# Gated FFT filter and state-space mixer on one core: first token results in freed rows of x, decay tables emitted earlier, a doubled recurrence PSUM, a narrower table and an earlier diagonal

## The chip, the cores and the metric

The kernel runs on one core of a Trainium2 chip. The metric is the device time in microseconds (us) of one execution, lower is better. A profiled execution also has a span, from the first to the last recorded instruction, which is about 1.8 us shorter than its device time.

## The reference, cut to what matters

```python
# x: [1, 2048, 1024] bfloat16
g = sigmoid((x * gate_w).sum(-1, keepdims=True))
a = irfft2(rfft2(x) * (w_r + 1j * w_i))             # A: filter over tokens and features
# B: state-space recurrence over the 2048 tokens, 1024 complex states
Bu = x @ B_bar.T
h[t] = Lam_bar * h[t - 1] + Bu[t]
b = 2.0 * (h @ Cmat.T).real + x * Dskip
return g * a + (1 - g) * b
```

## The kernel before

TensorE, VectorE and ScalarE run in an order fixed by the program text (`manual_schedule` names these three engines). The SyncE queue is not among them: it issues its transfers one after another in an order that the build chose. In the kernel before, the store of A1(9) is written two steps ahead of the first transpose of C, and the trace shows it issued behind all sixteen. The parts that matter:

- *Front, 16 steps.* Step j transforms group j of x (its 128 rows 16p + j) along the features (`fd`, PSUM `ps_fd`), ScalarE copies it out (`X1`), a first token stage follows (`s1`, PSUM `ps_s`), and its result `A1` is stored to DRAM for the next stage.
- *Recurrence, 16 units.* Each unit is two half units of 32 matmuls (PSUM `psu`), each copied to SBUF by ScalarE; then VectorE rotates, scans and rotates back.
- *Bcol*, a small table that VectorE makes and that TensorE's product `zps` reads, after the front.
- *Early output tiles* `ps_y`, which start with a product with the diagonal table `dgD`.

```python
CT = [ctp.tile([P, 8, D], BF16, name=f"CT{ri}") for ri in range(2)]
xn = [CT[i // 4][:, 2 * (i % 4):2 * (i % 4) + 2, :] for i in range(8)]   # x lies here first, C^T later
psA = ...tile_pool(name="psA", bufs=2, space=PSUM)     # ps_fd, ps_s and others
psF = ...tile_pool(name="psF", bufs=1, space=PSUM)     # psu of the first units
psX = ...tile_pool(name="psX", bufs=2, space=PSUM)     # turns of x
# [cut]
def s1(j):
    X1 = X1s.pop(j)
    psa = psA.tile([P, 2, K], FP32, name="ps_s1", tag="ps")
    for r in range(2):
        for g in range(2):
            half = slice(64 * g, 64 * (g + 1))
            nc.tensor.matmul(psa[:, g, :], lhsT=T2_sb[half, j, r, :], rhs=X1[half, r, :], ...)
    A1 = A1_4[:, j % 4]                                # four buffers, used in turn
    (nc.vector.tensor_copy if j < 8 else nc.scalar.copy)(out=A1, in_=psa)
    nc.sync.dma_start(out=t1_w[j], in_=A1)             # its place in the SyncE queue is chosen by the build
    if j % 4 == 0 and j:
        keep_A1(j - 4)                                 # column 0 of four results
# [cut] the loop over the front
    if j >= 8:
        halves(ssm, 1)                                 # one half unit of matmuls
    if j >= 9:
        vector(4.2)                                    # some VectorE pieces of the recurrence
    if j == 11:
        xctx.close()                                   # psF and psX end
        pools["u"] = ...tile_pool(name="psU", bufs=2, space=PSUM)
# [cut] after the front
for v, n in (("w", 4), ("a", 1), ...):
    assert step() == v                                 # "a": Bcol, "z": zps
    for i in range(n):
        halves(ssm, 1)
        vector(3.0)
        if v == "w" and i == 1:
            nc.vector.tensor_mul(out=fft["dgD"], ...)
```

## Time and profile before

| | before |
|---|---|
| median of the three timed runs | 346.62 us (346.26 to 347.94) |
| profiled execution | 348.02 us, span 346.2 us, mean granted clock 0.993 |
| TensorE busy | 328.4 us, 95% of the span |
| longest TensorE gap after the start | 3.39 us, at 44.98 us |
| next | 1.94 us, for `dgD`, at 105.47 us |

The chain that ended last is TensorE in 73% of its length, so the busy shares say little more than "TensorE". The useful question is where TensorE does not work, and the view of busy time by stretches answers it. The columns are the stretch, its length, then busy time and instructions of each engine, the granted clock (TensorE's clock as a share of its full one), the DMA share (rough, it can exceed 1) and the rate in GB/s. Two stretches of the kernel before:

```profile
40.00:60.00 20.00, 15.68 (x104) 9.68 (x105) 10.05 (x22) 11.06 (x17) 1.83 (x3) 0.91 1.08 212
...
80.00:110.00 30.00, 27.96 (x228) 20.00 (x229) 29.00 (x43) 10.22 (x12) 0.00 (x0) 1.00 0.71 186
```

In the first stretch TensorE (15.68 of 20 us, at a granted clock of 0.91) and VectorE (10.05 of 20 us) both stand still for part of the time. In the second TensorE loses 2.0 us while VectorE is full.

### The profile page before, as it was taken

The numbers are of one execution on the slowest core, as the hardware profiler recorded it, in microseconds if no ns is written. First come the engines' busy times: TensorE is split into PE (matmuls) and PEld (weight loads), VectorE is DVE, ScalarE is ACT, GpSimd is POOL, SyncE is SP. The second block draws the span as 40 slices with busy tenths as digits, with TensorE's granted clock in tenths as the row PEclk, the third lists the DMA queues.
The fourth block names the chain that finished last, engine by engine and source line by source line (L and its number), as shares of the span: only waits on it lengthen the run. The fifth ranks groups of instructions, "written<-read, shape, count | busy, mean of one in ns | idle before, by whom it ended". The sixth has DMA issues, their size and how long they took to land.

```text
span 346.2 us, 6210 instructions
## 1 busy us (share of the span) xinstructions
PE 328.4 (95%) x2414; PEld 213.7 (62%) x2446; DVE 289.0 (83%) x447; ACT 169.8 (49%) x214; POOL 33.6 (10%) x64
## 2 busy tenths in 40 slices
PE   8989578999998999999999999999999999999995
PEld 4445255666865775665748475858955885665552
DVE  2659356999999998999999999999990797999951
ACT  3698558775341225566646562456631333424410
POOL 1382010230000000000000000000000002112220
PEclk9999989999999999999999999999999999999999
DMA  7999999999882123889989953967302109956695
GB/s 251 407 224 130 220 220 211 214 151 252 278 196 35 61 91 92 225 225 249 276 182 287 271 170 95 247 158 203 91 2 91 62 0 149 181 98 98 113 141 166
DMA packets 83582, 58.97 MB, mean 170 GB/s; under 512 B 54329, under 2 KB 74305, under 8 KB 83425
## 3 DMA queue, kind: packets, MB, share of 16 engines
q1 hardware_dynamic: 80304, 55.90, 65.1%
q0 software_dynamic: 3168, 2.66, 7.9%
q8 instruction: 19, 0.31, 0.4%
q14 instruction: 11, 0.08, 0.1%
q10 hardware_dynamic: 80, 0.01, 0.0%
HBM read 30.76 MB, written 17.83 MB: 140 GB/s over the span
## 4 chain that ended last, share of the span: by engine, by line
PE 73%; DVE 17%; ACT 4%; SPq 2%; issue 2%; DMA 1%; DVEq 0%; ACTq 0%
PE ps_y L567 27%; PE psu L300 23%; PE ps_h L567 4%; DVE h L275 4%; PE ps_id L598 4%; PE ps_is L481 2%; SPq L205 2%; PE ps_is L506 2%; PE ps_is L482 2%; PE ps_y L571 2%; PE ps_s L457 2%; PE ps_fd L336 2%; PE psw L668 1%; DVE h L287 1%; ACT xQ L654 1%
## 5 line engine op out<-in xcount | busy, mean ns | idle before, releaser
L300 PE MATMUL psu<-xQ,BT 128*128 128x256 bf16 x1024 | 117.5, 274 | 1.5 <-ACT h L302 1.0
L300 PEld LDWEIGHTS <-BT 128*128 128x128 bf16 x1024 | 99.5, 98 | 19.1 <-issue 4.8
L567 PE MATMUL ps_y<-CT,h 128*128 128x512 bf16 x436 | 99.5, 379 | 0.6
L567 PEld LDWEIGHTS <-h 128*128 128x128 bf16 x512 | 49.5, 98 | 55.3
L275 DVE TENSOR_TENSOR_SCAN h<-rz,h 128x1024 bf16<-128x1024 f32 x32 | 72.6, 2293 | 0.3
L302 ACT CAST h<-psu 128x1024 bf16<-128x1024 f32 x32 | 32.4, 1011 | 58.2 <-PE psu L300 58.2
L613 POOL DMA_DIRECT2D BT<-y_scratch x10 | 11.9, 1194 | 241.1 <-DVE BT L607 233.5
L585 ACT ACTIVATE ye<-ps_y,omg 128x512 f32<-128x512 f32 x20 | 12.7, 684 | 43.5 <-PE ps_y L571 28.7
L336 PE MATMUL ps_fd<-G_sb,preT 128*128 128x512 bf16 x119 | 29.3, 379 | 2.9 <-ACT X L339 2.4
L262 DVE TENSOR_TENSOR su<-h,tab 128x2048 bf16<-128x2048 bf16 x16 | 19.6, 1222 | 3.5 <-ACT h L302 2.8
L336 PEld LDWEIGHTS <-preT 128*128 128x128 bf16 x128 | 12.1, 97 | 15.9 <-issue 3.8
L459 ACT CAST X<-ps_s 128x1024 bf16<-128x1024 f32 x16 | 16.2, 1015 | 8.7 <-PE ps_s L457 8.7
L287 DVE TENSOR_TENSOR h<-h,tab 128x2048 bf16<-128x2048 bf16 x16 | 20.0, 1249 | 0.5
L263 DVE TENSOR_TENSOR h<-h,tab 128x2048 bf16<-128x2048 bf16 x16 | 19.6, 1225 | 0.8
L339 ACT CAST X<-ps_fd 128x1024 bf16<-128x1024 f32 x16 | 16.2, 1013 | 8.1 <-PE ps_fd L336 7.4
L286 DVE TENSOR_TENSOR sg<-h,tab 128x2048 bf16<-128x2048 bf16 x16 | 19.5, 1219 | 0.1
L351 DVE CAST A<-ps_s 128x1024 bf16<-128x1024 f32 x8 | 9.8, 1222 | 8.6 <-DMA turn_scratch<-A 6.8
L654 ACT COPY xQ<-pt 128x1024 bf16<-128x1024 bf16 x16 | 15.8, 1020 | 1.8 <-PE pt L653 1.7
L508 ACT CAST ZT<-ps_is 128x1024 bf16<-128x1024 f32 x16 | 15.5, 1023 | 2.2 <-PE ps_is L506 2.2
L484 ACT CAST C<-ps_is 128x1024 bf16<-128x1024 f32 x16 | 16.1, 1008 | 0.0
L598 PE MATMUL ps_id<-raw,ZT 128*128 128x256 bf16 x128 | 15.9, 273 | 0.0
L567 PE MATMUL ps_h<-CT,h 128*128 128x512 bf16 x62 | 14.4, 379 | 0.1
(184 smaller groups left out, 364.7 us busy)
## 6 DMA issues: line engine op xcount, KB each, us to landing
y_scratch<-ye SPq DMA_DIRECT2D x20, 256.0 KB, 2.8
CT<-in_A_x_dram SPq DMA_DIRECT2D x8, 512.0 KB, 6.2
turn_scratch<-A SPq DMA_DIRECT2D x16, 256.0 KB, 3.7
Bb<-turn_scratch SPq DMA_DIRECT2D x16, 256.0 KB, 3.8
turn_scratch<-C SPq DMA_DIRECT2D x16, 256.0 KB, 3.6
raw<-turn_scratch SPq DMA_DIRECT2D x16, 256.0 KB, 4.0
Wb<-in_A_w_r_dram SPq DMA_DIRECT2D x32, 127.8 KB, 4.0
Wb<-in_A_w_i_dram SPq DMA_DIRECT2D x32, 127.8 KB, 3.7
```

The lines of the kernel that those rows point to most:

```text
L262: nc.vector.tensor_mul(out=su, in0=u[:, ::-1], in1=bc(1))
L263: nc.vector.tensor_mul(out=u, in0=u, in1=bc(0))
L275: nc.vector.tensor_tensor_scan(out=seg, data0=rz[:, js].rearrange("p j t -> p (j t)"), data1=seg, initial=0.0, op0=ALU.mult, op1=ALU.add)
L286: nc.vector.tensor_mul(out=sg, in0=u[:, ::-1], in1=bc(3))
L287: nc.vector.tensor_mul(out=u, in0=u, in1=bc(2))
L300: nc.tensor.matmul(psu[:, j, :], lhsT=BT[4 * q + j][:, ri, d8, :], rhs=x_t[:, d8, :, :, 8 * c:8 * (c + 1)], start=(d8 == 0), stop=(d8 == 7))
L302: nc.scalar.copy(out=u[:, ri].rearrange("p b (q j) -> p b q j", j=32), in_=psu.rearrange("p b (j q) -> p b q j", j=32))
L336: nc.tensor.matmul(ps[:, cls, :], lhsT=preTs[j][:, 4 * cls + d4, :], rhs=G_sb[:, cls, d4, :], start=(d4 == 0), stop=(d4 == 3))
L339: nc.scalar.copy(out=X1.rearrange("p r (i c) -> p r i c", c=2), in_=ps.rearrange("p c (r i) -> p r i c", r=2))
L567: nc.tensor.matmul(psy, lhsT=hs[c, jb // 4][:, ri, jb % 4, P * tq:P * (tq + 1)], rhs=CT[ri][:, jb, 512 * dh:512 * (dh + 1)], start=(i == 0 ...
L598: nc.tensor.matmul(pse[:, slot, :], lhsT=ZT_t[:, i, tb, :], rhs=fft["Gi"][:, i, :], start=(kb == 0), stop=(kb == 1))
L654: nc.scalar.copy(out=xQ[:, :, j, :].rearrange("p d (g q) -> p d g q", g=2), in_=pt.rearrange("p d (q g) -> p d g q", g=2))
```

## The change

The intent: let no store hold up the front, load less, and take two smaller waits away. Five edits:

1. Results of steps 0 to 7 go into rows of x that have been turned already (`CT[0]`), so that no result has to wait for an older one's store.
2. The decay tables `rz` are emitted on GpSimd right after their input.
3. The recurrence gets two PSUM buffers at step 7, before its first unit, instead of step 11; the gate's sums move to another pool for that.
4. The table T2 has 192 columns instead of 256 for each step, as one of its four blocks of 64 columns stood there twice.
5. The diagonal table `dgD` is made earlier on VectorE.

```diff
-        T2=b16(np.stack([np.concatenate([Tc, -Ts], axis=2), np.concatenate([Ts, Tc], axis=2)], axis=2)),
+        T2=b16(np.concatenate([Ts, Tc, -Ts], axis=2)),
 [cut: the rz copies move from the table builder to just after r_sb]
-                    nc.tensor.matmul(psa[:, g, :], lhsT=T2_sb[half, j, r, :], rhs=X1[half, r, :],
+                    nc.tensor.matmul(psa[:, g, :], lhsT=T2_sb[half, j, 64 - 64 * r:192 - 64 * r], rhs=X1[half, r, :],
-            A1 = A1_4[:, j % 4]
+            A1 = CT[0][:, j, :].rearrange("p (g k) -> p g k", g=2) if j < 8 else A1_4[:, j % 4]
-            if j % 4 == 0 and j:
+            if j in (8, 12):
                 keep_A1(j - 4)
         def keep_A1(j):
+            if j < 8:
+                nc.vector.tensor_copy(out=Acol[:, :, 0:8].rearrange("p g j -> p j g"), in_=CT[0][:, :, 0:D:K])
+                return
-        zps = psX.tile([P, K], FP32, name="zps_g", tag="pt")
+        zps = psA.tile([P, K], FP32, name="zps_g", tag="ps")
-        if j == 11:
+        if j == 7:
             xctx.close()
+            if v == "w" and i == 0:
+                nc.vector.tensor_mul(out=fft["dgD"], ...)
             halves(ssm, 1)
             vector(3.0)
-            if v == "w" and i == 1:
-                nc.vector.tensor_mul(out=fft["dgD"], ...)
```

More of the change, by code (lines that the diff above doesn't have):

```diff
@@ L191 @@
     raw = t3p.tile([P, 6 * D], BF16, name="raw")
-    fft["T2"] = raw[:, 0:4 * D].rearrange("p (j t m) -> p j t m", t=2, m=P)
+    fft["T2"] = raw[:, 0:3 * D].rearrange("p (j m) -> p j m", m=192)
     def load_x(i):
@@ L213, in make_tab @@
             nc.vector.tensor_scalar_mul(out=ang[:, j], in0=tau_f, scalar1=thp[:, 2 * jp + j:2 * jp + j + 1])
-            jb = 2 * jp + j
-            nc.gpsimd.tensor_copy(out=rz[:, jb, :], in_=r_sb[:, jb:jb + 1].to_broadcast([P, TC]))
-            nc.gpsimd.memset(rz[:, jb, 0:1], 0.0)
         sn_f = tmp.tile(sh, FP32, name="sn_f")
@@ L804 @@
     nc.scalar.activation(out=r_sb, in_=are, func=ACT.Exp)
+    for jb in range(8):
+        nc.gpsimd.tensor_copy(out=rz[:, jb, :], in_=r_sb[:, jb:jb + 1].to_broadcast([P, TC]))
+        nc.gpsimd.memset(rz[:, jb, 0:1], 0.0)
     tau_f = tmp.tile([P, TC], FP32, name="tau_f")
@@ L877 @@
         for i in range(n):
+            if v == "w" and i == 0:
+                nc.vector.tensor_mul(out=fft["dgD"], in0=ident.unsqueeze(1).to_broadcast([P, 8, P]),
+                                     in1=vecT[:, 3].unsqueeze(2).to_broadcast([P, 8, P]))
             if v == "w" and i == 3:
@@ L881 @@
             vector(3.0)
-            if v == "w" and i == 1:
-                nc.vector.tensor_mul(out=fft["dgD"], in0=ident.unsqueeze(1).to_broadcast([P, 8, P]),
-                                     in1=vecT[:, 3].unsqueeze(2).to_broadcast([P, 8, P]))
     for g in range(16):
```

## The prediction

> **What bounds the kernel now.** I read the page first (busy shares, the 40 slices, the chain that ended last), then the TensorE timeline with its gaps, then VectorE, ScalarE and the SyncE queue in the same windows. From the page, busy time and the engine shares of the chain:
>
> ```profile
> PE 328.4 (95%) x2414; PEld 213.7 (62%) x2446; DVE 289.0 (83%) x447; ACT 169.8 (49%) x214; POOL 33.6 (10%) x64
> ...
> PE 73%; DVE 17%; ACT 4%; SPq 2%; issue 2%; DMA 1%; DVEq 0%; ACTq 0%
> ```
>
> TensorE does work in 328.4 of 346.2 us, so all its gaps together are 17.8 us. In time order the chain is TensorE alone from 105.5 us to the end (in all that time the only listed waits are 0.53 and 0.23 us), and a mixture of VectorE, ScalarE and a DMA between 12 and 105 us. So what counts is by how much TensorE is shifted to the left by the time it reaches 105 us, and whether it keeps that afterwards. TensorE between 37 and 57 us (start, duration, operation, in brackets the idle before it and what ended it):
>
> ```profile
> 37.65 0.61 PE L348 MATMUL ps_s<-X,raw 64*128 64x512 bf16 x4
> 39.71 1.89 PE L336 MATMUL ps_fd<-G_sb,preT 128*128 128x512 bf16 x8 [1.45 <-ACT X L339]
> 44.98 1.04 PE L348 MATMUL ps_s<-X,raw 64*128 64x512 bf16 x4 [3.39 <-DVE A L351]
> 45.95 4.64 PE L300 MATMUL psu<-xQ,BT 128*128 128x256 bf16 x32
> 50.43 1.89 PE L336 MATMUL ps_fd<-G_sb,preT 128*128 128x512 bf16 x7
> 52.25 0.60 PE L348 MATMUL ps_s<-X,raw 64*128 64x512 bf16 x4
> 53.58 3.65 PE L300 MATMUL psu<-xQ,BT 128*128 128x256 bf16 x32 [0.73 <-ACT h L302]
> ```
>
> The largest gap of the kernel, 3.39 us, waits for VectorE to empty the other PSUM buffer. The VectorE and SyncE-queue timelines say why VectorE was late: it may not overwrite one of four A1 buffers until the store of four steps before has landed, and that store sat in the in-order SyncE queue behind the transposes of B.
>
> ```profile
> 36.37 1.22 DVE L351 CAST A<-ps_s 128x1024 bf16<-128x1024 f32 x1 [2.25 <-DMA turn_scratch<-A]
> 43.70 1.23 DVE L351 CAST A<-ps_s 128x1024 bf16<-128x1024 f32 x1 [4.51 <-DMA turn_scratch<-A]
> ...
> 34.72 5.38 SPq L205 DMA_TRANSPOSE BT<-in_B_B_re_dram  x4
> 40.20 0.53 SPq L353 DMA_DIRECT2D turn_scratch<-A  x1
> ```
>
> The data of that store were in SBUF at 21.5 us; it was issued at 40.2. The second place is the first early output tile, which waits for the diagonal table dgD, made by VectorE late in its order:
>
> ```profile
> 104.20 1.22 DVE L883 TENSOR_TENSOR dgD<-ident,vecT 128x1024 bf16<-128x1024 bf16 x1
> ...
> 105.47 0.38 PE L571 MATMUL ps_y<-dgD,xs 128*128 128x128 bf16 x4 [1.94 <-DVE dgD L883]
> ```
>
> **What the Trainium skill says.** "TensorE: Matmul & The Clock Gate", section "What's actually happening": after an idle window of about 3.4 us the array goes back to half its clock, and needs about as long of sustained work to come back. The trace agrees: after the 3.39 us gap four first-stage matmuls take 1.04 us instead of 0.60, the next 32 take 4.64 us instead of the 3.67 of all later groups, and the granted clock is 0.83 between 42 and 52 us. "Perfetto Trace Analysis", section "What 'DMA-bound' means": a sequencer that is solid DMA slices is busy making descriptors. The SyncE queue agrees: from 48.0 to 74.7 us it issues sixteen transposes of C at about 1.3 us each with stores between, so a store's place in that queue decides when its buffer is free. "GPSIMD Engine Reference", section "1. Specifications": GpSimd shares its SBUF interfaces with VectorE; no part of this case turns on it, as shown next.
>
> **The change part by part.**
> *Decay tables.* A comparison of the two built programs shows the same GpSimd stream in the same order. Before, the eight copies (about 0.43 us each) already run between 11.1 and 14.3 us, straight after r_sb. Worth 0.
> *T2 from 256 to 192 columns.* 16 x 64 columns x 128 partitions x 2 bytes = 0.25 MB of 1 MB less, in a stretch where the queues moved about 400 GB/s (10 to 20 us): an estimated 0.6 us of transfer. But TensorE's gaps from 12 to 36 us end on ScalarE (X and xQ), not on a load. I count 0.1.
> *A1 of steps 0 to 7 in rows of x already turned.* Waits of 2.25 and 4.51 us go. Replayed in order: A1(6) follows its matmuls (35.0) and ends at 36.3. The tables of 37.6 still wait for ScalarE; the fold of 38.4 ends at 39.2, A1(7) runs 39.2 to 40.4 instead of 43.7 to 44.9. The transform at 39.71 still waits for ScalarE (1.45 stays) and ends at 41.55, so the first-stage group starts there instead of at 44.98: 3.4. With no long gap the clock stays up: 0.44 for that group (1.04 - 0.60), 0.97 for the next (4.64 - 3.67), together 1.4. The same copy of the zero column also stops waiting for ScalarE (2.36 us on VectorE).
> *Two recurrence PSUM buffers from the first unit.* The wait of 0.73 at 53.58 goes: only that one, because later units have other matmuls between them. The gate's sums move to the other pool; by the order that buffer is emptied (X) well before. TensorE arrives at 57 us earlier by 3.4 + 1.4 + 0.7 = **5.5 us**.
> *dgD ahead.* It moves in front of the second scan, at 99.2 instead of 104.2, so its 1.94 us wait goes: 5.5 + 1.9 = **7.4 us** for TensorE at 105.5. VectorE's total work is the same.
>
> Now VectorE, which is dense from 58.4 us (9.8 of 10 us in each of the next windows). Its first recurrence piece starts at 58.39, after ScalarE has copied the second half unit at 57.27. ScalarE's table pieces follow VectorE's angles, which move from 46.74 to 42.26 (-4.5); after that copy queue ScalarE is free at 52.3 and TensorE's half unit is done at 51.7, so the copy starts at 52.3 (-5.0). **VectorE moves 5.0 us, TensorE 7.4.** The difference meets at a small table:
>
> ```profile
> 111.64 0.17 DVE L411 TENSOR_SCALAR Bcol<-Bcol 32x64 bf16<-32x64 bf16 x1
> ...
> 113.22 0.56 PE L417 MATMUL zps<-Bcol,K_sb 32*128 32x16 bf16 x16
> ```
>
> TensorE needs Bcol at 113.22 - 7.4 = 105.8, VectorE has it at 111.8 - 5.0 = 106.8: about 1.0 us comes back as a wait. Further on the states of the recurrence are ready 12 us or more before use (for the third early tile, 120.5 against 132.9), and VectorE itself waits for TensorE and ScalarE at 121.5 and 134.5, so it catches up. Sum: 7.4 - 1.0 + 0.1 = 6.5; I take off 0.3 for the store wait below: **6.2 us, 340.4 us.**
>
> **The rivals.**
> 1. *The store wait comes back later.* Steps 8 to 15 still share four buffers. A1(13) may only be written when the store of A1(9) has landed, and that store stays behind all sixteen transposes of C: issued at 74.8, landed about 78.5 by the median of 3.7, and A1(13) at 79.5 just cleared it. TensorE 5.5 us earlier wants it at 74.0; the SyncE queue, bound by its own issuing, moves only about 0.7 us earlier, and its transposes into the first half of C now first wait for the stores of A1(5) to A1(7). ScalarE then stands some 3.7 us, but TensorE has 4.9 us of other matmuls before it needs that PSUM buffer. By this count it is touched, not stopped; each us later costs one, though part of it is then taken out of the 1.0 at Bcol. If the queue is 3 us later than I think: 342.5 to 343.
> 2. *Transfers limit the early stretch anyway.* The DMA share is full until 87 us. Against it: B's rows land before TensorE asks (no TensorE gap ends on them), and the first xs is issued at 91.0 and read at 103.2. If it did hold, the gain would be 2 to 4 us: 343 to 345.
> 3. *VectorE is the bound throughout.* It is 96% busy from 120 to 250 us (124.6 of 130); then the gain is VectorE's 5.0 us, 341.6. Against it: the slack of 12 us and its idle 9.8 us near 260, which waits for TensorE.
> 4. *All of it arrives*: 346.6 - 7.4 - 0.6 = 338.6, if VectorE also moves fully.
>
> **Range and chances.** 338.6 (rival 4) to 343.0 (rival 1) with the centre 340.4. Faster by over 2% needs 339.7, which is 0.7 below the centre: 0.27. Slower by 2% has no mechanism here: 0.01. The rest is within 2%.
>
> **What would show it.** Right: no VectorE wait on the stores of steps 0 to 7; no TensorE gap over 2 us between 37 and 60 us and a granted clock near 1.0 there; the half unit groups of 32 at 3.67 us from the first; no gap on dgD; a new gap of about 1 us before zps at some 106 us; recurrence on VectorE starting near 53.4; from 110 us on the same spacing as before, shifted by 6 us. Wrong: a ScalarE cast of A1 waiting for a store around 74 to 78 us with TensorE behind it, an early tile waiting for C or xs, or the clock dropping elsewhere.

## The result, and the profile after

The changed kernel took 341.35 us (median of 4 runs, 340.97 to 342.74); the kernel before, on the same chip, 347.11 us (4 runs, 346.26 to 347.94). The ratio is 0.984, with a 95% interval of 0.980 to 0.988: faster, but within the 2% that counts as the same. (Ratios here are the mean time of one kernel's fast runs over that of the other's of the same rounds, so not quite the ratio of the medians.) The median lies 0.95 us above the predicted 340.4. The two profiled executions took 348.02 and 340.97 us, a difference of 7.05 us.

The page of the changed kernel, busy shares and engine shares of the chain:

```profile
PE 326.4 (96%) x2414; PEld 212.4 (63%) x2446; DVE 288.6 (85%) x446; ACT 169.7 (50%) x214; POOL 33.6 (10%) x64
...
PE 73%; DVE 19%; ACT 6%; issue 2%; DVEq 0%; ACTq 0%
```

The SyncE queue (SPq) and the DMA have left the chain. TensorE's gaps sum to 339.2 - 326.4 = 12.8 us instead of 17.8; the other 2.0 us of the shorter span are busy time, of which 1.4 us are the two groups after the old gap, no longer at a slow clock. The same two stretches as before:

```profile
40.00:60.00 20.00, 19.75 (x165) 12.71 (x166) 14.29 (x28) 15.67 (x24) 2.82 (x5) 1.00 1.09 219
...
80.00:110.00 30.00, 29.16 (x259) 22.12 (x258) 29.03 (x44) 9.80 (x12) 0.00 (x0) 1.00 0.82 200
```

TensorE's 20 us from 40 to 60 us now hold 19.75 us of work at a granted clock of 1.00. One by one, the TensorE timeline of the changed kernel (start, duration, operation, idle before it and what ended it):

```profile
37.22 0.60 PE L345 MATMUL ps_s<-X,raw 64*128 64x512 bf16 x4
39.42 1.89 PE L333 MATMUL ps_fd<-G_sb,preT 128*128 128x512 bf16 x8 [1.59 <-ACT X L336]
41.23 0.61 PE L345 MATMUL ps_s<-X,raw 64*128 64x512 bf16 x4
41.77 3.67 PE L297 MATMUL psu<-xQ,BT 128*128 128x256 bf16 x32
45.28 1.89 PE L333 MATMUL ps_fd<-G_sb,preT 128*128 128x512 bf16 x7
47.10 0.60 PE L345 MATMUL ps_s<-X,raw 64*128 64x512 bf16 x4
47.64 3.67 PE L297 MATMUL psu<-xQ,BT 128*128 128x256 bf16 x32
...
97.79 0.40 PE L571 MATMUL ps_y<-dgD,xs 128*128 128x128 bf16 x4 [0.24 <-DMA xs<-in_A_x_dram]
...
106.17 0.54 PE L417 MATMUL zps<-Bcol,K_sb 32*128 32x16 bf16 x16 [0.55 <-DVE Bcol L410]
...
262.16 10.64 PE L297 MATMUL psu<-xQ,BT 128*128 128x256 bf16 x96 [0.53 <-ACT ye L585]
```

Read it against the seven lines of before in the prediction. The 3.39 us gap ahead of the first-stage group and the 0.73 us gap ahead of the second half unit are gone; the group takes 0.61 us instead of 1.04, the half unit 3.67 instead of 4.64. The wait for `dgD` has become one of 0.24 us for `xs`. A new wait of 0.55 us stands before `zps`. The line at 262.16 is at 269.22 in the kernel before, with the same wait of 0.53 us: a shift of 7.06 us, as at `zps` (113.22 - 106.17 = 7.05). Nothing is gained or lost after 106 us.

VectorE in the changed kernel, the copies of A1(6) and A1(7) and the first recurrence piece:

```profile
34.76 1.23 DVE L348 CAST CT<-ps_s 128x1024 bf16<-128x1024 f32 x1 [1.11 <-PE ps_s L345]
...
38.82 1.21 DVE L348 CAST CT<-ps_s 128x1024 bf16<-128x1024 f32 x1
...
52.86 1.23 DVE L259 TENSOR_TENSOR su<-h,tab 128x2048 bf16<-128x2048 bf16 x1 [2.18 <-ACT h L299]
```

No copy of steps 0 to 7 waits for a store; the A1(7) copy starts at 38.82 instead of 43.70. The first recurrence piece, in the kernel before:

```profile
58.39 1.23 DVE L262 TENSOR_TENSOR su<-h,tab 128x2048 bf16<-128x2048 bf16 x1 [2.82 <-ACT h L302]
```

VectorE's recurrence starts 5.53 us earlier, TensorE by then 5.93 us (the transform at 57.07 is now at 51.14).

The store wait did come back, on ScalarE, which copies A1 from step 8 on. ScalarE, A1(12) and A1(13), in the changed kernel:

```profile
69.83 1.01 ACT L348 CAST A<-ps_s 128x1024 bf16<-128x1024 f32 x1 [1.32 <-DMA turn_scratch<-A]
...
77.30 1.01 ACT L348 CAST A<-ps_s 128x1024 bf16<-128x1024 f32 x1 [3.69 <-DVE h L266]
```

The profile puts the second wait down to a VectorE instruction, as the last semaphore that came. By the order, this copy reuses the buffer of A1(9), whose store is the first of a group of four that the queue issued at 74.12 us; the stores of this stretch took 3.0 us or more to land, which gives 77.1 us or later. The experiment with seven buffers below agrees. TensorE's next first-stage group, at 78.36 us, has no gap before it: the wait is hidden.

One side remark: in the kernel before, `keep_A1(j - 4)` is called after step j has already overwritten the first of the four buffers, so by reading the program the kept columns of steps 0, 4 and 8 are those of steps 4, 8 and 12; in the changed kernel this is left for step 8 alone.

### The profile page after: what moved, and what is told of

Its sections match the earlier page's. It is cut to its first block, busy times and chain, and to the rows that moved or that the text cites. A ratio compares the mean times of both kernels' runs of the same rounds, so it can differ in the third digit from the quotient of the medians.

```text
span 339.2 us, 6204 instructions
## 1 busy us (share of the span) xinstructions
PE 326.4 (96%) x2414; PEld 212.4 (63%) x2446; DVE 288.6 (85%) x446; ACT 169.7 (50%) x214; POOL 33.6 (10%) x64
## 4 chain that ended last, share of the span: by engine, by line
PE 73%; DVE 19%; ACT 6%; issue 2%; DVEq 0%; ACTq 0%
PE ps_y L567 26%; PE psu L297 22%; PE ps_h L567 4%; DVE h L272 4%; PE ps_id L598 4%; PE ps_fd L333 3%; PE ps_is L481 2%; PE ps_is L506 2%; PE ps_is L482 2%; PE ps_y L571 2%; ACT xQ L654 2%; PE ps_s L457 2%; ACT X L336 1%; DVE h L260 1%; DVE su L259 1%
## 5 line engine op out<-in xcount | busy, mean ns | idle before, releaser
L598 PEld LDWEIGHTS <-ZT 128*128 128x128 bf16 x128 | 12.4, 98 | 2.2
```

What stands on the lines that cost most here:

```text
L598: nc.tensor.matmul(pse[:, slot, :], lhsT=ZT_t[:, i, tb, :], rhs=fft["Gi"][:, i, :], start=(kb == 0), stop=(kb == 1))
```

## The experiments

**Theory:** the gain is the store waits of the rows (with the clock that they cost) plus the wait for `dgD`, less what VectorE, moved by less than TensorE, hands back at Bcol. **Rivals:** the returned store wait takes part of the gain (prediction's rival 1); the transfers or T2 limit the front (rival 2); VectorE bounds throughout, so that TensorE waits alone are worth nothing (rival 3).

All medians are of six runs, beside eleven of the kernel before of the same rounds: 347.61 us for the first four experiments, 347.11 for the next four, 348.17 for the last four. All results were correct. The experiments and the changed kernel were timed in different sets of rounds, so a difference between them of some 0.5 us is not told apart.

Two of the edits also change the order that the build gives the SyncE queue, as the traces show. With the narrow T2 the second store stands behind three transposes of B instead of two. With the rows, all eight imaginary parts of C are issued ahead of the real ones, which go into those rows. So the runs with and without these two edits compare the edit together with its order; e1 and e3 keep the order of before.

| kernel | edit | median us | ratio to before (95%) |
|---|---|---|---|
| e1 | before + dgD early | 345.63 | 0.9945 (0.9914 to 0.9977) |
| e2 | before + rows | 343.43 | 0.9890 (0.9859 to 0.9921) |
| e3 | before + doubled PSUM | 348.38 | 1.0020 (0.9994 to 1.0047) |
| e4 | before + narrow T2 | 347.52 | 1.0004 (0.9967 to 1.0041) |
| e5 | after, without rows | 344.48 | 0.9939 (0.9897 to 0.9980) |
| e6 | after, dgD late | 342.91 | 0.9878 (0.9852 to 0.9903) |
| e7 | after, single PSUM | 341.69 | 0.9840 (0.9814 to 0.9865) |
| e8 | e5 + work in the gap | 345.58 | 0.9955 (0.9917 to 0.9994) |
| e9 | after, seven A1 buffers | 341.28 | 0.9805 (0.9774 to 0.9836) |
| e10 | after, Bcol first | 341.43 | 0.9803 (0.9771 to 0.9834) |
| e11 | after, tables earlier | 346.10 | 0.9949 (0.9920 to 0.9978) |
| e12 | e9 + e10 + e11 | 346.51 | 0.9959 (0.9926 to 0.9992) |

### One part alone, on the kernel before

**e1, dgD early.**

```diff
+            if v == "w" and i == 0:
+                nc.vector.tensor_mul(out=fft["dgD"], ...)
             halves(ssm, 1)
             vector(3.0)
-            if v == "w" and i == 1:
-                nc.vector.tensor_mul(out=fft["dgD"], ...)
```

> The kernel before with only dgD moved ahead. Theory (TensorE is shifted up to the point where VectorE's Bcol stops it): the 1.94 us wait goes, but TensorE then reaches zps at 111.3 us and Bcol is still ready at 111.8, so about 0.5 comes back: 1.4 us less, 345.7 us. Rival A (each wait counts in full): 1.9 less. Rival B (VectorE is the bound): no change, 347.1.

Measured: 2.0 us faster. The wait for `dgD` is gone, and a new one stands before `zps` (TensorE timeline of e1):

```profile
111.39 0.54 PE L417 MATMUL zps<-Bcol,K_sb 32*128 32x16 bf16 x16 [0.80 <-DVE Bcol L410]
```

So a TensorE wait alone is worth time, which speaks against a bound by VectorE throughout; and VectorE takes back what it is behind, here 0.80 us. The medians do not tell the 1.4 us of the theory from the 1.9 of rival A. The store wait is that of before (4.51 us on VectorE), and so is the gap in TensorE's timeline of e1:

```profile
44.37 0.64 PE L348 MATMUL ps_s<-X,raw 64*128 64x512 bf16 x4 [3.38 <-DVE A L351]
```

**e2, rows.** `keep_A1` goes with it as in the change; T2 and the rest stay as before.

```diff
-            A1 = A1_4[:, j % 4]
+            A1 = CT[0][:, j, :].rearrange("p (g k) -> p g k", g=2) if j < 8 else A1_4[:, j % 4]
-            if j % 4 == 0 and j:
+            if j in (8, 12):
```

> The kernel before with only A1 of steps 0 to 7 in rows of x. Theory: the waits of 2.25, 4.51 and 3.39 us and the slow clock go; the single recurrence buffer now costs about 1.0 us at the second half unit instead of 0.73; dgD still waits about 1.6 to 1.9 us. About 4.7 us less: 342.4 us. Rival A (the clock and the wait add up and nothing comes back): 5.2 or more less. Rival B (the store wait only moves to steps 12 and 13 and stops TensorE there): 2 us less or nothing.

Measured: 4.2 us faster, 1.0 us short of the expected 342.4. The returned store wait is exposed here. ScalarE, the SyncE queue and TensorE in e2, each view in turn:

```profile
80.04 1.01 ACT L351 CAST A<-ps_s 128x1024 bf16<-128x1024 f32 x1 [4.95 <-DMA turn_scratch<-A]
```

```profile
76.63 2.51 SPq L353 DMA_DIRECT2D turn_scratch<-A  x4
```

```profile
81.10 0.61 PE L348 MATMUL ps_s<-X,raw 64*128 64x512 bf16 x4 [1.20 <-ACT A L351]
```

The four stores were issued at 76.63 us, against 74.12 in the changed kernel, and TensorE stood for 1.20 us. So rival 1 is a real mechanism, on the edge of hurting. e2 has the wide T2; in the five kernels with rows, the narrow T2 and the table pieces of before (the changed one, e6, e7, e9, e10) the group was issued between 72.98 and 74.67. That the narrower table, or the order of the queue that comes with it, is what moved the group is an inference from these profiles, not shown.

**e3, doubled PSUM.**

```diff
-        zps = psX.tile([P, K], FP32, name="zps_g", tag="pt")
+        zps = psA.tile([P, K], FP32, name="zps_g", tag="ps")
-        if j == 11:
+        if j == 7:
             xctx.close()
```

> The kernel before with only the two recurrence buffers from the first unit on (gate in the other pool). Theory: the 0.73 us wait goes for TensorE, but VectorE starts only 0.5 earlier because ScalarE is busy with table pieces, and dgD is waited for after it: 0.5 us less, 346.6 us, not told from noise. Rival: 0.7 less.

Measured: no gain (348.38; all six runs had a mean granted clock of 0.990 to 0.995, none 1.0). In its profiled execution the half-unit wait is gone and the gap for A1(7) is short, but TensorE, earlier, waits longer for the unmoved `dgD`. TensorE in e3, then the SyncE queue's issue of the store that A1(7) waits for:

```profile
43.09 0.61 PE L348 MATMUL ps_s<-X,raw 64*128 64x512 bf16 x4 [0.97 <-DVE A L351]
...
103.47 0.58 PE L571 MATMUL ps_y<-dgD,xs 128*128 128x128 bf16 x4 [3.52 <-DVE dgD L883]
```

```profile
38.30 0.53 SPq L353 DMA_DIRECT2D turn_scratch<-A  x1
```

The wait for `dgD` is 3.52 us instead of 1.94, and the four small matmuls behind it take 0.58 us instead of 0.38: the clock has dropped. TensorE reaches this wait 3.6 us earlier than in the profile of before; only 0.7 of that is the PSUM wait, most of the rest is the shorter store wait of this execution, with the clock that stayed up. A wait removed ahead of a fixed later wait is not a gain, and here it cost the clock.

**e4, narrow T2.**

```diff
-    fft["T2"] = raw[:, 0:4 * D].rearrange("p (j t m) -> p j t m", t=2, m=P)
+    fft["T2"] = raw[:, 0:3 * D].rearrange("p (j m) -> p j m", m=192)
 [cut: the table and its slices as in the change]
```

> The kernel before with only the narrower T2 table (0.25 MB less to load). Theory: TensorE's gaps before 36 us end on ScalarE, so 0 to 0.3 us less. Rival (transfers limit the early stretch): 0.6 to 1 us less, and the stores of A1 land earlier so that the 4.51 us wait shrinks by as much.

Measured: no difference. 0.25 MB less to load, with the order of the queue that comes with it, gives nothing that the runs can show, which speaks against rival 2 in this form. VectorE's wait for the store did shrink, to 3.15 us from 4.51, as the rival expected, but e3 has 2.10 us with the wide table. Its TensorE timeline is of use for another reason:

```profile
43.37 0.69 PE L348 MATMUL ps_s<-X,raw 64*128 64x512 bf16 x4 [2.02 <-DVE A L351]
44.00 5.20 PE L300 MATMUL psu<-xQ,BT 128*128 128x256 bf16 x32
```

The gap was shorter in this execution (2.02 us), and the clock dropped all the same: 5.20 us for the half unit.

### One part taken out of the changed kernel

**e5, without the rows** (A1 back in four buffers, `keep_A1` as before).

```diff
-            A1 = CT[0][:, j, :].rearrange("p (g k) -> p g k", g=2) if j < 8 else A1_4[:, j % 4]
+            A1 = A1_4[:, j % 4]
```

> The changed kernel with the four A1 buffers back for all steps. Theory: the waits on the stores, the 3.4 us gap and the slow clock return; what is left of the gain is 0.5 (buffers) plus up to 1.9 (dgD), limited by Bcol: 1.9 us under the kernel before, 345.2, so the rows are worth about 5 of the 7 us. Rival (dgD and the PSUM buffers carry the gain): 343 or less.

Measured: 344.48, 3.1 us slower than the changed kernel. The profiled execution had a gap of 2.11 us ahead of the first-stage group, yet the half unit took 3.67 us:

```profile
43.23 0.61 PE L345 MATMUL ps_s<-X,raw 64*128 64x512 bf16 x4 [2.11 <-DVE A L348]
43.77 3.67 PE L297 MATMUL psu<-xQ,BT 128*128 128x256 bf16 x32
```

**e6, dgD late.**

```diff
-            if v == "w" and i == 0:
+            if v == "w" and i == 1:
 [cut: the product of dgD, again after vector(3.0)]
```

> The changed kernel with dgD back in its old place. Theory: VectorE starts the recurrence 5.5 us earlier than before the change, dgD with it, so TensorE waits for it about 2.3 us and the whole is 5.5 us under the kernel before: about 1.5 above the changed kernel, 342.8. Rival (dgD's wait is covered by the wait at Bcol anyway): within 0.6 of the changed kernel.

Measured: 342.91, 1.6 us slower; `dgD` is waited for 2.69 us, and the granted clock stays at 1.00 between 96 and 108 us.

**e7, single PSUM until step 11.**

```diff
-        zps = psA.tile([P, K], FP32, name="zps_g", tag="ps")
+        zps = psX.tile([P, K], FP32, name="zps_g", tag="pt")
-        if j == 7:
+        if j == 11:
```

> The changed kernel with one recurrence buffer until step 11 again. Theory: the second half unit waits about 1.0 us for ScalarE's copy (47.6 to 48.7), VectorE starts 0.7 to 1.0 later: 0.7 us above the changed kernel, 342.0. Rival (only the 0.73 of before is at stake, and it is hidden): no difference.

Measured: 341.69, only 0.3 us slower, although a wait of 0.98 us is back at 48.35 us; the medians do not tell this from nothing.

**e8: is it the gap or what stands behind it that drops the clock?** e5 with matmuls whose result nobody reads, put into the gap:

```diff
+                if j == 8:
+                    wps = pools["u"].tile([P, 4, TC], FP32, name="wps", tag="psu")
+                    for i in range(14):
+                        nc.tensor.matmul(wps[:, 0:2].rearrange("p a t -> p (a t)"), lhsT=ident, rhs=xQ[:, i % 8, 0:4, :], start=True, stop=True)
```

> The kernel of the run with four A1 buffers and all else changed, plus 14 useless matmuls of 512 columns (about 3.0 us) in the gap while TensorE waits for A1. Theory of the clock: the wait of about 3.4 us before the first-stage group stays in sum, but that group takes 0.60 instead of 1.04 us and the 32 after it 3.67 instead of 4.64, granted clock 1.0; the total stays within 0.5 us of that run, because ScalarE's table pieces and then Bcol stop TensorE afterwards. Rival (those matmuls were slow for another reason, such as the transfers): they stay at 1.04 and 4.64.

TensorE in e8:

```profile
41.58 3.18 PE L780 MATMUL wps<-xQ,ident 128*128 128x512 bf16 x14
45.20 0.61 PE L345 MATMUL ps_s<-X,raw 64*128 64x512 bf16 x4 [0.44 <-DVE A L348]
45.74 3.67 PE L297 MATMUL psu<-xQ,BT 128*128 128x256 bf16 x32
```

In this execution VectorE waited 3.09 and 3.86 us for the two stores, together about as long as in the kernel before, and both groups ran at the full clock. That fits idle time as what costs the clock, and so do the other profiles: taken in windows of 2 us from 2 to 336 us, the granted clock falls under 0.99 only at TensorE gaps of 2.02 to 4.91 us and behind them. It is not proved by this pair, as e5, with the gap left open, kept its clock too. The total is inconclusive: 344.14 to 348.13 us, with a median 1.1 us above that of e5 where 0.5 was expected at most; three of six runs of each have a mean granted clock of 0.998 or more. In e8 a wait came later, at Bcol, which the expectation had named as the next stop, and the clock dropped there:

```profile
111.81 0.56 PE L414 MATMUL zps<-Bcol,K_sb 32*128 32x16 bf16 x16 [2.09 <-DVE Bcol L407]
```

The granted clock was 0.51 between 112 and 114 us.

### Does a further step gain?

**e9, seven A1 buffers for steps 8 to 15**, so that no copy of steps 8 to 14 waits for a store.

```diff
-    A1_4 = gta.tile([P, 4, 2, K], BF16, name="A1", bufs=1)
+    A1_4 = gta.tile([P, 7, 2, K], BF16, name="A1", bufs=1)
-            A1 = ... if j < 8 else A1_4[:, j % 4]
+            A1 = ... if j < 8 else A1_4[:, (j - 8) % 7]
 [cut: keep_A1 follows the new places]
```

> The changed kernel with seven instead of four A1 buffers for steps 8 to 15. Theory: ScalarE's waits on the stores at steps 12 and 13 (1.32 and 3.69 us in the changed kernel) vanish, and the total stays within 0.5 us, 341.3, because TensorE did not wait for them. Rival (the returned store wait delays the recurrence): 1 us or more less.

Measured: 341.28. ScalarE's A1 copies at 69.12 and 74.23 us have no wait, and the time is that of the changed kernel. The returned store wait lies beside the path, in the changed kernel as it stands.

**e10, Bcol ahead of the recurrence pieces.**

```diff
-            vector(3.0)
+            vector(0.0 if v == "w" and i == 3 else 6.0 if v == "a" else 3.0)
```

> The changed kernel with Bcol made by VectorE ahead of the three join operations before it (1.5 us earlier). Theory (the last 0.55 us gap is VectorE's lag at Bcol): the gap goes, 0.5 us less, 340.8. Rival (VectorE, now later with the recurrence, stops TensorE elsewhere): no change or slower.

TensorE in e10 has no wait at `zps`:

```profile
104.95 0.56 PE L417 MATMUL zps<-Bcol,K_sb 32*128 32x16 bf16 x16
```

Its profiled span, 338.0 us, is the shortest of all, but that was also its fastest run; the median, 341.43, is not told apart from the changed kernel's, so the expected 0.5 us is not seen.

**e11, table pieces moved**: one fewer is done by the end of steps 6 and 7, to let the casts of X go first, and one more from step 9 on:

```diff
-        front(0 if j < 4 else 1 if j < 6 else 2 if j < 10 else 3)
+        front(0 if j < 4 else 1 if j < 7 else 2 if j < 8 else 3)
```

> The changed kernel with the rotation-table pieces of steps 6 and 7 pushed behind the casts of X. Theory: TensorE's waits of 0.68 and 1.59 us on X shrink by 0.8 or more together, but what arrives is what VectorE gains: 0.3 to 0.9 us less, 340.8. Rival (the pieces bunch up ahead of the copy of the first recurrence unit): VectorE starts later and the total is 0.5 or more longer.

A miss: 346.10. The second wait on X did shrink (0.80 us instead of 1.59) and the recurrence did start earlier (52.15 instead of 52.86 us), but ScalarE and TensorE in e11 show a new wait:

```profile
62.22 0.63 ACT L818 ACTIVATE rot_kk<-ang 128x512 f32<-128x512 f32 x1 [7.36 <-DVE ang L816]
```

```profile
64.80 1.04 PE L345 MATMUL ps_s<-X,raw 64*128 64x512 bf16 x4 [4.91 <-ACT zsb L698]
65.77 5.48 PE L297 MATMUL psu<-xQ,BT 128*128 128x256 bf16 x32
```

ScalarE's next table piece, now a step earlier, needs angles which VectorE makes behind a scan and other recurrence pieces; ScalarE stands for 7.36 us in front of the copy that empties TensorE's PSUM buffer; TensorE stands for 4.91 us and then runs a half unit in 5.48 us instead of 3.67.

**e12, all three.**

> Seven A1 buffers, Bcol earlier and the table pieces later together. Theory: with the stop at Bcol gone TensorE keeps what it gains in front: 1.2 us less than the changed kernel, 340.1. Rival: VectorE stops it elsewhere, within 0.3 of the best single one.

A miss for the same reason: 346.51, with the same gap of 4.90 us at 64.68 us. No version was clearly faster than the changed kernel.

## Why the prediction was right

The chance given to "within 2%" was 0.72, the range 338.6 to 343.0 holds the 341.35, and the centre was 0.95 us low. Step by step, with the traces of before and after:

| step of the prediction | predicted us | measured us |
|---|---|---|
| front, before the transform at 39.71 | -0.1 | -0.29 |
| gap for A1(7) | -3.4 | -3.39 |
| clock after the gap | -1.4 | (1.04 + 4.64) - (0.61 + 3.67) = -1.40 |
| second PSUM buffer | -0.7 | -0.73 |
| dgD | -1.9 | 1.94 - 0.24 = -1.70 |
| VectorE's start | -5.0 | -5.53 |
| returned at Bcol | +1.0 | +0.55 |
| allowance for the store wait | +0.3 | 0 |
| TensorE from zps on | -6.2 | -7.05 |

- **The mechanism held.** TensorE moved by more than VectorE, the two met at Bcol, and from there everything kept its spacing. The front's 0.29 us is not an effect to count: in the profiles of the experiments that leave it alone, this transform starts anywhere from 39.1 to 40.2 us.
- **VectorE's start was 0.5 us too cautious**, of which the front is 0.3. With VectorE earlier, less came back at Bcol. e10 shows that even this remainder is worth no more than the spread of the runs.
- **Rival 1 was seen rightly.** ScalarE stood 3.69 us against the 3.7 predicted, and TensorE did not. e2 shows the case where it does hurt, 1.20 us, and e9 that in the changed kernel nothing is left to gain there. The 0.3 us taken off for it was not due.
- **Rival 2, as far as e4 tests it, and rival 3 fell**: e4 (no gain from the smaller load) and e1 (2.0 us from a TensorE wait alone). The decay tables stand in the same GpSimd order in both programs, and GpSimd is busy for 33.6 us in both; no run tried them alone.
- **What was sized wrongly is the term "the first-stage group starts there instead of at 44.98: 3.4" with its 1.4 of clock, taken as a property of the kernel.** It varies from one execution to the next. e1 and e3 have the order of the queue of before. In e1 the wait is there again (4.51 us on VectorE, a gap of 3.38). In e3 the queue issued the store at 38.30 us instead of 40.20, VectorE's wait was 2.10 us, TensorE's gap 0.97, and the clock stayed up there. The timed runs say the same: of the 33 of the kernel before beside the experiments, 12 have a mean granted clock of 0.998 or more, against 0.993 in the profile; of the 34 runs of the kernels with rows (without e11 and e12, which have another long gap), 32 have it. What the drop costs in the whole stays open: the median of those 12 runs is 347.2 us, that of the 13 at 0.993 to 0.995 is 347.6.
- **The nearness of the number is in part luck.** With the measured sizes the steps give about 7.0 us, which is what lies between the two profiled executions. But the one of before lies 0.91 us above its median and that of the changed kernel 0.38 below, so the medians differ by 347.11 - 341.35 = 5.76 us. The predicted 6.2 is too small for the one and 0.44 too large for the other. The remaining 0.49 us of the miss is the base, 346.62 for what was 347.11 with one run more.
- **One reading in the prediction is wrong, without weight for its sum.** At 21.5 us the data of A1(2) were in SBUF. The store issued at 40.20 is that of A1(3), whose copy in the kernel before runs from 26.59 to 27.81 us.
- **Parts do not have fixed prices.** Alone on the kernel before, rows, dgD, PSUM and T2 gave -4.2, -2.0, +0.8 and -0.1 us; taken out of the changed kernel, rows, dgD and PSUM cost 3.1, 1.6 and 0.3. The PSUM buffer is the clearest: 0.73 us in the trace, nothing in either comparison. In e3 its gain went into the wait for `dgD`; in the changed kernel VectorE's start and Bcol are a likely limit to what TensorE keeps; the record does not show it for this part.

What stays open: whether the narrower T2, or the order that comes with it, is what kept the queue 2.5 us ahead of that in e2, and why the SyncE queue, with the same transfers in the same order, reaches one store 1.9 us earlier in one execution than in another.

## What to carry to other kernels

When a wait is a buffer that a queued store still holds, look first for storage that is already dead (here rows of the input) before adding buffers, and then follow the wait to where the next shared buffers show it again. Predict with the shift of each engine separately, and find the instruction where the slower-moving engine hands the difference back. Before pricing a gap from one trace, see how far that execution's own time lies from the median: a wait for a transfer may be half as long in the next run, and a gap whose removal only lengthens a later wait is worth nothing.

## What the Trainium skill lacked or had wrong

- "TensorE: Matmul & The Clock Gate", section "Why this matters for your kernels", advises no idle gaps of more than about 3 us. That is too generous as a safe limit here: in e4 a gap of 2.02 us (after one of 1.59 us, with 1.89 us of matmuls between) was followed by a half unit of 5.20 us instead of 3.67, and in e8 one of 2.09 us by a granted clock of 0.51, while in e5 a gap of 2.11 us after the same 1.59 and 1.89 us, and in e6 one of 2.69 us, left the clock up. The page's remark in the section "What's actually happening" that the window runs freely would allow such a difference, which no run here tests; the advice does not carry it over.
- "DMA: Bandwidth & Descriptors", section "Latency and other measured facts", has a latency on average and one under load, but no spread between executions for a store that is queued behind other transfers. Here one 256 KB store was issued at 40.20 us in the kernel before and at 38.30 in e3, with the same transfers in the same order ahead of it; VectorE's wait for it was 4.51 and 2.10 us, and the kernel before spread from 345.6 to 349.3 us.
